# Luna attention and a SmeLU feed-forward on one core: query parts ahead of the values, batch 1's first keys ahead of the weights, orders set anew

## The chip, the core and the metric

One core of one Trainium2 chip runs the whole program. The metric is the device time of one execution in microseconds (us), the median of several. Six engines or queues matter here: TensorE (PE in the profile, with its weight loads as PEld), VectorE (DVE), ScalarE (ACT), GpSimd (POOL), SyncE (SP), and the DMA engines that POOL and SP feed.

## The reference, cut to what matters

```python
def sm_attn(qq, kk, vv):
    s = scale * np.matmul(qq, kk.transpose(0, 1, 3, 2))
    a = np.exp(s - np.max(s, axis=-1, keepdims=True))
    return np.matmul(a / (np.sum(a, axis=-1, keepdims=True) + 1e-09), vv)
p_packed = sm_attn(p, k, v)               # 32 pack queries over 576 keys
out = sm_attn(q, p_packed, p_packed)      # 576 queries over 32 packed keys
x = out.transpose(0, 2, 1, 3).reshape(B * S, H * D)      # 4608 x 512
h = x @ w_in                                             # 512 x 2048
g = np.where(h >= 1, h, np.where(h <= -1, 0.0, (h + 1) ** 2 / 4))
return g @ w_out                                         # 2048 x 512
```

There are 8 batches of 8 heads, 576 tokens, 64 wide. Inputs and output are float32; the kernel multiplies in bfloat16.

## The kernel before, in words

**Tiling.** A batch goes through two stages. The attention stage turns the keys (line 432, tile `tp`, copied to `kT`), takes the scores of the 32 pack queries (line 459, `sp`), their exponentials on ACT (line 462, `ex`), and packs the values (lines 479 and 485, `pk`; from it `ppT` and the reciprocals `rs`). Then come the scores of the real queries against the packed keys (`s`, line 513, and for batch 0 line 591), their exponentials `eT`, the sums `sm` by a matmul with blocks of ones (lines 528 and 597), the inverse of the sums as `ln` and then `rc` on ACT, and the weights `A` on DVE. The packed values are multiplied into `w_in` beforehand: `M` is `ppT` times a block of columns of `w_in` (line 659, tile `mp`, cast to `M` by DVE or ACT), so that a hidden tile of 128 features is `h = M x A` (line 733). The SmeLU of a hidden tile is three instructions: `x` out of PSUM on ACT (line 738), a clamp on DVE (line 743) or ACT (line 745), and a product into `hT` on DVE (line 748). The output tile `o` of 128 tokens sums 16 matmuls of `hT` with `w_out` (line 795); two batches make a pair of 9 output tiles.

**Batch 0** is done in smaller pieces, since everything waits for it: its queries are turned on PE in four pieces (line 582), by x (first or second part of the tokens) and g (four heads each); the hidden tiles whose number is in `HALVED` are made for each half of the tokens apart, the second half with a key that is `hx` later; `MERGED` names the x for which `ln` and `rc` of both g are one instruction; `SPLIT` names the blocks of `M` that are cast in two pieces. The first output tiles of the first pair are summed in two parts (`CUTS`): after that many of the 16 hidden tiles the sum is copied out (`part`, "parked") and added to the rest later (line 806).

**What sets the order.** A planner (`Plan`, `run`, `choose`) writes the instructions out for every engine. It has a cost for each kind of work (`C`), and among the tasks that can start it takes the one with the smallest key; the keys of a hidden tile are its batch plus a sixteenth for each tile, those of the attention work stand in the table `KEYS`, a row for each batch, and output tiles come last (100 and more). Its choice of engine for a copy (DVE or ACT) also follows its costs. On the chip each engine runs its list in order and waits where an input isn't there. Where the planner sees PE with nothing to do before the third output tile, it writes matmuls of zeros (line 870, 512 or 256 columns) into the list: they are work without a result.

**Loads.** POOL issues all input loads in one list: first those of `FIRST` (k, v and queries of batch 0, in parts), then those of `ORDER`, where `r` is the second query part of batch 0, `i` and a number a block of columns of `w_in`, `o` and a number a quarter of `w_out`, `k`, `q` and `v` loads of batch 1, `p` the rest of the pack queries. SP issues the stores of the output and, for later batches, transposes of q and k by DMA.

**PSUM** has three places `W` that everything but the output tiles passes through, and two places `O` for output tiles.

Of the kernel before, what the change touches and what calls it, by code (L numbers as in the profile page):

```python
# [13 lines left out]
         Tca=1.12, Tcd=0.75, ex=0.807, ppo=0.4, ppT=0.41, ppa=0.4, ppd=0.22, rs=0.165,  # L14
         eT=0.741, ln=0.651, rc=0.683, A=0.816, Mca=1.014, Mcd=1.223, x=0.651, ta=0.681, td=0.459, hT=0.757, oba=0.586, obd=0.69, hx=2.181,
         array=0.2, tell=0.04, lead=0.12, until=18.0, feed=0.2374, margin=0.3641, slack=0.1788, wake=1.2, warm=7.0, early=0.2216, wait=0.002722, p4=999.0, bk=115.3)
OVER = {"ACT": 0.104, "DVE": 0.083}
NW, NO, NX, NB = 3, 2, 5, 6
DW, FILL = 256, 512
CUTS = (4, 4, 8, 8)  # L20
PARTS = len(CUTS)

ORDER = 'r i0 i1 i4 o0 i2 q0 i3 k1 k0 o1 v q1 o2 o3 p'

FIRSTS = "kT0 kT1 sc0 sc1 pk0 pk1 q00 q01 q10 q11 s200 s201 s210 s211 sm00 sm01 sm10 sm11 M0 M1 M2 M3 M4".split()
UNITS = "kT0 kT1 qT0 qT1 sc0 sc1 pk0 pk1 s20 s21 sm0 sm1 M0 M1 M2 M3".split()
KEYS = [
# [187 lines left out]
def kernel(  # L215
# [10 lines left out]
    nc = tc.nc  # L226
# [9 lines left out]
    P = 128  # L236
# [10 lines left out]
    X = 2  # L247
# [20 lines left out]
    PE, ACT, DVE, DMA, SP = "PE", "ACT", "DVE", "DMA", "SP"  # L268
# [144 lines left out]
    def attention(b, key):  # L413
# [156 lines left out]
        def first_weights(deps, r):  # L570
# [37 lines left out]
            for x in range(X):  # L608
                boxes, own, cps = [{}, {}, {}], None, []
                for g in range(G):  # L610
                    t = add(PE, C["tp"] * 6, key["q%d%d" % (x, g)], [part_of["q", x, g]] + ([own] if g else []),
                            lambda x=x, g=g, bx=boxes[0]: turn(x, g, bx), takes=None if g else "W", readers=0 if g else 2, mode=1)
                    own = own or t
                    cps.append(both(lambda eng, x=x, g=g, bx=boxes[0]: copy(qT()[:, x, g * w:(g + 1) * w], bx["tp"][:, g, :w])(eng),
                                    C["Tca"] * 0.55, C["Tcd"] * 0.55, key["q%d%d" % (x, g)], [t], frees=own))
                    tq[x, g] = t
                own = None
                for g in range(G):
                    ky = key["s2%d%d" % (x, g)]
# [4 lines left out]
                    eTs[x, g] = add(ACT, C["eT"] * 0.6, ky, [t, r[g]], lambda eng, x=x, g=g, bx=boxes[1]: nc.scalar.activation(  # L624
                        eT(g)[:, x], bx["s2"][:, g, :HALF], AF.Exp, scale=rs()[:, g, 1:]), frees=own)
# [9 lines left out]
                for gs in ([slice(G)] if merged else [slice(g, g + 1) for g in range(G)]):  # L635
# [3 lines left out]
                    for g in range(G)[gs]:  # L639
                        As[x, g] = add(DVE, C["A"] * 0.56, key["sm%d%d" % (x, g)], made, lambda eng, x=x, g=g, bx=bx: nc.vector.scalar_tensor_tensor(  # L640
                            A()[:, g, x], eT(g)[:, x], rs()[:, g, :1], bx["rc"][:, g], ALU.mult, ALU.mult))
# [7 lines left out]
        def mk(f, deps):  # L649
# [15 lines left out]
            war = K.get((b - 2, "h"), [])  # L665
            part = {2: 0.56, 4: 1.0}[n // P] * (0.58 if len(gs) > 1 else 1.0)
            yield t, [both(lambda eng, g=g: copy(M()[:, g, cs], box["mp"][:, g, :n])(eng), C["Mca"] * part,
# [49 lines left out]
    def hidden_tile(b, fi, key, hs=None):  # L717
# [8 lines left out]
        xs = slice(hs[0], hs[-1] + 1)  # L726
        pa, pd = (1.0, 1.0) if n == X else (0.6, 0.56)

# [26 lines left out]
        war = [step_of[b // 2 - 1, i, fi] for i in range(lo, lo + 5)] if b > 1 else []  # L755
        t_ = add(DVE, C["hT"] * pd, key, [t_] + war, third, frees=x_)
        for x in hs:
# [143 lines left out]
```

## Time and profile before

| | before |
|---|---|
| median of 3 runs | 248.5 us (247.53 to 248.61) |
| the profiled execution's own time | 248.8 us |
| its span, first to last instruction | 247.0 us |
| mean granted TensorE clock | 0.979 |
| PE busy | 239.4 us (97%), 2221 matmuls |
| DVE busy, ACT busy | 175.3 us (71%), 185.2 us (75%) |
| POOL busy | 31.3 us (13%) |
| chain that ended last | PE 93%, DMA 3%, POOL, DVE and issue 1% each |

A busy PE is not a useful PE: the matmuls of zeros count as busy, and the ends of matmuls are modelled. So the page's 97% is read together with the groups by line (how many matmuls of zeros there are) and with the timeline of the first 30 us. Windows give the busy time of every engine in a stretch and the granted clock; rows of the timeline give start, duration, engine, line, tiles, count, and in brackets the idle time ahead and what ended it. The chain of waits, in order of time, gives the pieces on which the end hung.

### The profile page before, as it was taken

Reading aid. Unit: us, or ns where it says so; the run is one execution under the profiler, and the core shown is the slowest. Engines: PE = TensorE matmul, PEld = TensorE weight load, DVE = VectorE, ACT = ScalarE, POOL = GpSimd, SP = SyncE. Lnnn points to the kernel's source line nnn. Section 1 sums busy time; section 2 is a strip of 40 time slices with the busy share of each in tenths; the row PEclk is TensorE's granted clock in tenths of the full one; section 3 lists DMA queues with packets and bytes.
Section 4 is the critical chain, followed back from the end, with each engine's and each line's share of the span. In section 5 each row is a group of like instructions: output and inputs, shape, how many; then the busy total and the mean of one; then the engine's idle time right before and its main releaser. Section 6 shows DMA issues by size and latency. Waiting matters only on the chain.

```text
span 247.0 us, 5472 instructions
## 1 busy us (share of the span) xinstructions
PE 239.4 (97%) x2221; PEld 138.0 (56%) x2221; DVE 175.3 (71%) x314; ACT 185.2 (75%) x310; POOL 31.3 (13%) x46
## 2 busy tenths in 40 slices
PE   7689999999999999999999999999999999999994
PEld 2544567467644666357745664576545674476443
DVE  5336999689964699339987995389752997589400
ACT  3328998889967796769998997699466995899410
POOL 8652431210110102002101110000000000000000
PEclk9956999999999999999999999999999999999999
DMA  7999999999999999999999999634433102210232
GB/s 105 170 201 205 204 204 202 198 232 201 192 196 185 204 130 168 180 168 203 181 166 147 197 155 178 137 74 84 90 93 85 42 3 73 57 44 3 60 110 86
DMA packets 57258, 34.67 MB, mean 140 GB/s; under 512 B 30224, under 2 KB 52752, under 8 KB 57232
## 3 DMA queue, kind: packets, MB, share of 16 engines
q0 software_dynamic: 25984, 18.55, 53.2%
q1 hardware_dynamic: 31104, 15.70, 35.1%
q8 instruction: 17, 0.28, 0.5%
q10 hardware_dynamic: 144, 0.07, 0.1%
q14 instruction: 9, 0.07, 0.1%
HBM read 37.22 MB, written 9.44 MB: 189 GB/s over the span
## 4 chain that ended last, share of the span: by engine, by line
PE 93%; DMA 3%; POOL 1%; issue 1%; DVE 1%; ACT 0%; POOLq 0%
PE o L795 51%; PE h L733 26%; PE mp L659 4%; DMA v<-in_v_dram 3%; PE pk L479 2%; PE sp L459 2%; PE tp L432 1%; PE sm L528 1%; PE o L870 1%; PE s L513 1%; PE pk L485 1%; PE tp L582 1%; PE s L591 1%; PE sm L597 0%; POOL k L293 0%
## 5 line engine op out<-in xcount | busy, mean ns | idle before, releaser
L795 PE MATMUL o<-w_out_sb,hT 128*128 128x512 bf16 (+2 forms) x592 | 143.7, 374 | 0.0
L748 DVE SCALAR_TENSOR_TENSOR hT<-x 128x576 bf16<-128x576 f32 (+1 forms) x131 | 90.4, 737 | 0.6
L795 PEld LDWEIGHTS <-hT 128*128 128x128 bf16 x592 | 54.9, 98 | 53.9 <-issue 5.3
L738 ACT ACTIVATE x<-h 128x576 f32<-128x576 f32 (+1 forms) x131 | 76.5, 653 | 7.0 <-PE h L733 6.7
L733 PE MATMUL h<-A,M 128*128 128x288 bf16 x512 | 75.4, 287 | 0.0
L733 PEld LDWEIGHTS <-M 128*128 128x128 bf16 x512 | 49.9, 98 | 22.6 <-issue 1.3
L743 DVE TENSOR_SCALAR x<-x 128x576 f32<-128x576 f32 (+1 forms) x75 | 31.8, 450 | 9.8 <-ACT x L738 9.7
L745 ACT ACTIVATE x<-x 128x576 f32<-128x576 f32 (+1 forms) x56 | 37.5, 697 | 0.1
L375 DVE CAST M<-mp 128x1024 bf16<-128x1024 f32 (+1 forms) x16 | 17.9, 1122 | 13.3 <-PE mp L659 11.0
L375 ACT COPY ob<-o 128x512 f32<-128x512 f32 (+1 forms) x19 | 10.9, 575 | 20.7 <-PE o L795 20.2
L375 DVE COPY ob<-o 128x512 f32<-128x512 f32 (+1 forms) x14 | 9.5, 679 | 20.4 <-PE o L795 20.3
L375 ACT CAST M<-mp 128x1024 bf16<-128x1024 f32 (+2 forms) x20 | 17.6, 912 | 6.8 <-PE mp L659 6.5
L462 ACT ACTIVATE ex<-sp 96x768 bf16<-96x768 f32 x16 | 13.0, 815 | 4.0 <-PE sp L459 4.0
L548 DVE SCALAR_TENSOR_TENSOR A<-eT,rs,rc 128x576 bf16<-128x576 bf16 x12 | 9.8, 816 | 8.0 <-ACT rc L538 8.0
L293 POOL DMA_DIRECT2D k<-in_k_dram x10 | 7.6, 764 | 49.9 <-DMA kT<-k 36.8
L523 ACT ACTIVATE eT<-s,rs 128x576 bf16<-128x576 f32 x14 | 9.8, 746 | 2.7 <-PE s L513 2.4
L293 POOL DMA_DIRECT2D q<-in_q_dram x8 | 6.2, 777 | 42.6 <-DMA qT<-q 21.7
L533 ACT ACTIVATE ln<-sm 128x576 f32<-128x576 f32 x14 | 9.1, 652 | 3.1 <-PE sm L528 2.9
L870 PE MATMUL o<-zeros 128*128 128x512 bf16 (+1 forms) x25 | 10.2, 503 | 1.2 <-DVE zeros L281 1.2
L659 PE MATMUL mp<-w_in_sb,ppT 64*32 64x512 bf16 (+1 forms) x264 | 10.8, 380 | 0.0
L538 ACT ACTIVATE rc<-ln 128x576 f32<-128x576 f32 x14 | 9.6, 682 | 0.4
L459 PEld LDWEIGHTS <-kT 128*128 128x128 bf16 x192 | 7.8, 98 | 2.5 <-DVE kT L375 0.2
(61 smaller groups left out, 129.5 us busy)
## 6 DMA issues: line engine op xcount, KB each, us to landing
out_dram<-ob SPq DMA_DIRECT2D x23, 192.0 KB, 2.9
v<-in_v_dram POOLq DMA_DIRECT2D x7, 576.0 KB, 15.6
k<-in_k_dram POOLq DMA_DIRECT2D x6, 576.0 KB, 16.4
q<-in_q_dram POOLq DMA_DIRECT2D x6, 576.0 KB, 12.1
out_dram<-ob SPq DMA_DIRECT2D x22, 128.0 KB, 3.6
w_out_sb<-in_moe_w_out_dram POOLq DMA_DIRECT2D x4, 512.0 KB, 16.9
w_in_sb<-in_moe_w_in_dram POOLq DMA_DIRECT2D x3, 512.0 KB, 13.2
out_dram<-ob SPq DMA_DIRECT2D x22, 64.0 KB, 2.4
```

The costliest lines, as they stand in the source:

```text
L293: nc.gpsimd.dma_start(tok[nm, b][:, hs].rearrange("p h c d -> p h (c d)"), SRC[nm][b, hs].rearrange("h (p c) d -> p h (c d)", c=NC))
L375: return lambda eng: nc.vector.tensor_copy(out_, in_) if eng == DVE else nc.scalar.copy(out_, in_)
L459: nc.tensor.matmul(o[:, :, a], kT()[:, i, w:w + P], pT[:, b, h], start=True, stop=True)
L462: nc.scalar.activation(ex()[:, :, i].rearrange("p e x a n -> p e (x a n)"), box["sp"], AF.Exp, scale=scale)
L659: nc.tensor.matmul(mp[a * NP:(a + 1) * NP, g, :n], pp_of(y, h), w_in_sb[y * D:(y + 1) * D, h // 2, cs], start=True, stop=True)
L733: nc.tensor.matmul(h[:, hf, :HALF], T[b, "M"][:, g, fi * P:(fi + 1) * P], T[b, "A"][:, g, hf], start=(g == 0), stop=(g == G - 1))
L738: nc.scalar.activation(box["x"], box["h"][:, xs, :HALF], AF.Prelu, bias=-1.0, alpha=0.5)
L743: nc.vector.tensor_scalar(x, x, 1.0, 0.0, ALU.add, ALU.max)
L745: nc.scalar.activation(x, x, AF.Relu, bias=1.0)
L748: nc.vector.scalar_tensor_tensor(hT[:, fi, col + xs.start * HALF:col + xs.stop * HALF].rearrange("p (a t) -> p a t", a=n), box["x"], 1.0, ...
L795: nc.tensor.matmul(box["o", j, part][:, :cs.stop - cs.start], hT[:, fi, i * P:(i + 1) * P], w_out_sb[:, fi, cs], start=(fi == 0 or fi in c ...
L870: plan.run(lambda w: nc.tensor.matmul(o[:, :w], zeros[:, :P], zeros[:, :w], start=True, stop=True))
```

## The change

It changes numbers and tables, and the planner then writes other lists.

- `FIRST`: the two first query parts are loaded between k and v instead of after v.
- `ORDER`: the first half of batch 1's keys (`k0`) is loaded ahead of the first block of `w_in`; batch 1's other key half, its queries and two quarters of `w_out` change places further on.
- `CUTS`: output tiles 2 and 3 are parked after seven hidden tiles instead of eight.
- `HALVED`: a fourth hidden tile of batch 0 is made in halves. `hx`: the second halves have a key of 48 instead of 2 more, behind all other hidden tiles.
- `MERGED`: `ln` and `rc` of the first part of the tokens are made for each g apart. `SPLIT`: only the first block of `M` is cast in two pieces.
- Planner numbers: `feed`, `margin`, `slack`, `early`, `wait`, and the costs of pieces (0.55 to 0.6, 0.6 to 0.675 and so on); all of `KEYS`.

```diff
-         ... hx=2.181,
-         ... feed=0.2374, margin=0.3641, slack=0.1788, ..., early=0.2216, wait=0.002722, p4=999.0, bk=115.3)
+         ... hx=48.25,
+         ... feed=0.2568, margin=0.2281, slack=0.3077, ..., early=0.2764, wait=0.01662, p4=999.0, bk=999.0)
-CUTS = (4, 4, 8, 8)
+CUTS = (4, 4, 7, 7)
-ORDER = 'r i0 i1 i4 o0 i2 q0 i3 k1 k0 o1 v q1 o2 o3 p'
+ORDER = 'r k0 i0 i1 i4 o0 i2 k1 i3 o1 v q0 o2 q1 o3 p'
 KEYS = [
-    [3.797, -2.654, -2.321, 4.058, -3.234, -2.701, ...
+    [-3.469, -3.796, -3.804, -6.263, -4.244, -5.278, ...
...
-SPLIT = ((0, 0), (0, 1), (0, 2))
+SPLIT = ((0, 0),)
-FIRST = "k0 k1 v0 v1 q00 q01"
+FIRST = "k0 k1 q00 q01 v0 v1"
-FLOW = {"k0": 1.48, "k1": 1.52, "v0": 1.5, "v1": 1.46, "q00": 0.8, "q01": 0.8, "r": 1.6, "in0": 2.25, "in1": 1.33}
+FLOW = {"k0": 1.48, "k1": 1.52, "q00": 0.8, "q01": 0.8, "v0": 1.5, "v1": 1.46, "r": 1.56, "in0": 1.5, "in1": 2.0}
-HALVED = (0, 1, 2)
-MERGED = (0, 1)
+HALVED = (0, 1, 2, 3)
+MERGED = (1,)
...
-                                    C["Tca"] * 0.55, C["Tcd"] * 0.55, key["q%d%d" % (x, g)], [t], frees=own))
+                                    C["Tca"] * 0.6, C["Tcd"] * 0.6, key["q%d%d" % (x, g)], [t], frees=own))
...
-        pa, pd = (1.0, 1.0) if n == X else (0.6, 0.56)
+        pa, pd = (1.0, 1.0) if n == X else (0.63, 0.62)
```

The lists themselves move most at the start. First POOL, which issues the loads, from the first loads to the first block of `w_in` (a minus is the list before, a plus the new one; line 293 loads k or v, line 340 a query part, `masks.py` builds the identity for the transposes):

```order
 L293 DMA k<-in_k_dram 96x4x384 x2
-L293 DMA v<-in_v_dram 96x4x384
+L340 DMA q<-in_q_dram 96x4x192
 masks.py:197 MEMSET ident 128x128
 masks.py:199 ISA
 masks.py:199 AFFINE_SELECT ident<-ident 128x128
-L293 DMA v<-in_v_dram 96x4x384
-L340 DMA q<-in_q_dram 96x4x192 x2
+L340 DMA q<-in_q_dram 96x4x192
+L293 DMA v<-in_v_dram 96x4x384 x2
 L340 DMA q<-in_q_dram 96x8x192
+L293 DMA k<-in_k_dram 96x4x384
```

The two query parts pass the two value halves, and a key half of batch 1 now stands ahead of the first weights.

Then ACT, from batch 0's exponentials of the real scores to its first hidden tiles. Before (numbers tell the tiles apart):

```order
L624 ACTIVATE eT_301<-s2_285,rs_227 128x288
L602 ACTIVATE ln_332<-sm_299 128x576
L624 ACTIVATE eT_292<-s2_334,rs_227 128x288
L624 ACTIVATE eT_301<-s2_334,rs_227 128x288
L607 ACTIVATE rc_349<-ln_332 128x576
L375 CAST M_362<-mp_352 128x256
L602 ACTIVATE ln_365<-sm_347 128x576
L607 ACTIVATE rc_381<-ln_365 128x576
L375 CAST M_362<-mp_372 128x256
L738 ACTIVATE x_392<-h_384 128x288
```

And now:

```order
L602 ACTIVATE ln_337<-sm_333 128x288
L607 ACTIVATE rc_344<-ln_337 128x288
L624 ACTIVATE eT_293<-s2_339,rs_256 128x288
L602 ACTIVATE ln_337<-sm_333 128x288
L624 ACTIVATE eT_318<-s2_339,rs_256 128x288
L607 ACTIVATE rc_344<-ln_337 128x288
L602 ACTIVATE ln_385<-sm_371 128x576
L375 CAST M_401<-mp_375 128x256
L607 ACTIVATE rc_404<-ln_385 128x576
L462 ACTIVATE ex_413<-sp_387 96x3x256
L738 ACTIVATE x_417<-h_407 128x288
```

`ln` and `rc` of the first part stand there twice, half as wide, and the exponential of batch 1's first scores (`ex_413`) stands ahead of the first hidden tile's `x`.

Last DVE, from batch 0's turned queries to its weights `A`:

```order
-L375 COPY qT_95<-tp 128x576 x4
-L375 CAST M<-mp 128x256
-L640 SCALAR_TENSOR_TENSOR A<-eT,rs,rc 128x288 x2
+L375 COPY qT_95<-tp 128x576 x2
+L640 SCALAR_TENSOR_TENSOR A<-eT,rs,rc 128x288
+L375 COPY kT_94<-tp 128x1152
+L640 SCALAR_TENSOR_TENSOR A<-eT,rs,rc 128x288
 L375 CAST M<-mp 128x256
 L640 SCALAR_TENSOR_TENSOR A<-eT,rs,rc 128x288 x2
```

The copy of batch 1's first turned keys (`kT_94`) now stands between the two weights `A` of the first part; the other two query copies went ahead, behind batch 0's own keys.

On PE the matmuls are the same but for zeros: before there are 20 of 512 and 5 of 256 columns, now 23 and 4. Up to the place where PE makes three whole hidden tiles of batch 0 in a row (12 matmuls of line 733) for the first time, it now also has 12 transposes of batch 1's keys (line 432) and 12 of its scores (line 459), and one output matmul (line 795) less. Batch 0's first query transposes (24 of line 582) stand ahead of its second scores; before they stood behind both `pk`.

More of the change, by code (lines that the diff above doesn't have):

```diff
@@ L14 @@
          Tca=1.12, Tcd=0.75, ex=0.807, ppo=0.4, ppT=0.41, ppa=0.4, ppd=0.22, rs=0.165,
-         eT=0.741, ln=0.651, rc=0.683, A=0.816, Mca=1.014, Mcd=1.223, x=0.651, ta=0.681, td=0.459, hT=0.757, oba=0.586, obd=0.69, hx=2.181,
-         array=0.2, tell=0.04, lead=0.12, until=18.0, feed=0.2374, margin=0.3641, slack=0.1788, wake=1.2, warm=7.0, early=0.2216, wait=0.002722, p4=999.0, bk=115.3)
+         eT=0.741, ln=0.651, rc=0.683, A=0.816, Mca=1.014, Mcd=1.223, x=0.651, ta=0.681, td=0.459, hT=0.757, oba=0.586, obd=0.69, hx=48.25,
+         array=0.2, tell=0.04, lead=0.12, until=18.0, feed=0.2568, margin=0.2281, slack=0.3077, wake=1.2, warm=7.0, early=0.2764, wait=0.01662, p4=999.0, bk=999.0)
 OVER = {"ACT": 0.104, "DVE": 0.083}
@@ L623, in first_weights @@
                     K.setdefault((b, "s2"), []).append(t)
-                    eTs[x, g] = add(ACT, C["eT"] * 0.6, ky, [t, r[g]], lambda eng, x=x, g=g, bx=boxes[1]: nc.scalar.activation(
+                    eTs[x, g] = add(ACT, C["eT"] * 0.675, ky, [t, r[g]], lambda eng, x=x, g=g, bx=boxes[1]: nc.scalar.activation(
                         eT(g)[:, x], bx["s2"][:, g, :HALF], AF.Exp, scale=rs()[:, g, 1:]), frees=own)
@@ L639, in first_weights @@
                     for g in range(G)[gs]:
-                        As[x, g] = add(DVE, C["A"] * 0.56, key["sm%d%d" % (x, g)], made, lambda eng, x=x, g=g, bx=bx: nc.vector.scalar_tensor_tensor(
+                        As[x, g] = add(DVE, C["A"] * 0.63, key["sm%d%d" % (x, g)], made, lambda eng, x=x, g=g, bx=bx: nc.vector.scalar_tensor_tensor(
                             A()[:, g, x], eT(g)[:, x], rs()[:, g, :1], bx["rc"][:, g], ALU.mult, ALU.mult))
@@ L665, in mk @@
             war = K.get((b - 2, "h"), [])
-            part = {2: 0.56, 4: 1.0}[n // P] * (0.58 if len(gs) > 1 else 1.0)
+            part = {2: 0.57, 4: 1.0}[n // P] * (0.63 if len(gs) > 1 else 1.0)
             yield t, [both(lambda eng, g=g: copy(M()[:, g, cs], box["mp"][:, g, :n])(eng), C["Mca"] * part,
@@ L755, in hidden_tile @@
         war = [step_of[b // 2 - 1, i, fi] for i in range(lo, lo + 5)] if b > 1 else []
-        t_ = add(DVE, C["hT"] * pd, key, [t_] + war, third, frees=x_)
+        t_ = add(DVE, C["hT"] * (1.0 if n == X else 0.59), key, [t_] + war, third, frees=x_)
         for x in hs:
```

16 rows, old and new, of the table KEYS are left out of this document.

## The prediction

> **What bounds the kernel now.** I read the page's first part, then the busy times by stretch, cut at the places where the granted clock changes, then the chain of waits of the first 40 us.
>
> ```profile
> PE 239.4 (97%) x2221; PEld 138.0 (56%) x2221; DVE 175.3 (71%) x314; ACT 185.2 (75%) x310; POOL 31.3 (13%) x46
> ```
>
> ```profile
> 6.10:9.50 3.40, 2.43 (x50) 1.92 (x47) 1.65 (x4) 1.05 (x2) 2.87 (x4) 1.00 1.22 157
> 9.50:12.90 3.40, 2.20 (x50) 1.57 (x50) 0.94 (x6) 1.06 (x3) 1.90 (x3) 1.00 1.50 186
> 12.90:16.30 3.40, 2.65 (x29) 1.38 (x30) 1.17 (x3) 0.97 (x2) 1.86 (x4) 0.50 1.46 199
> 16.30:19.70 3.40, 3.20 (x44) 1.56 (x40) 0.82 (x2) 1.75 (x5) 1.26 (x2) 0.50 1.25 205
> 19.70:23.10 3.40, 3.40 (x26) 1.27 (x19) 2.69 (x7) 3.02 (x7) 1.26 (x2) 0.50 1.25 207
> 23.10:26.50 3.40, 3.40 (x29) 1.90 (x28) 3.37 (x7) 2.76 (x8) 0.99 (x2) 0.99 1.27 203
> 26.50:30.00 3.50, 3.50 (x30) 2.07 (x29) 3.47 (x9) 3.39 (x8) 1.59 (x2) 1.00 1.29 205
> 30.00:40.00 10.00, 10.00 (x116) 6.79 (x114) 9.80 (x17) 9.45 (x16) 3.45 (x5) 1.00 1.28 205
> 50.00:244.00 194.00, 193.86 (x1722) 112.72 (x1716) 140.52 (x238) 151.71 (x252) 9.61 (x12) 1.00 0.80 129
> ```
>
> The columns are the stretch, its length, PE, PEld, DVE, ACT, POOL, the granted clock, the DMA share and GB/s. From 50 us on PE is busy 193.86 of 194.00 us: no order of the same matmuls can win more than the missing 0.14 us there. What can be won lies ahead, where PE waits or multiplies zeros. Those are counted by group:
>
> ```profile
> L870 PE MATMUL o<-zeros 128*128 128x512 bf16 x20 | 9.0, 539 | 1.2 <-DVE zeros L281 1.2
> L870 PE MATMUL o<-zeros 128*128 128x256 bf16 x5 | 1.8, 360 | 0.0
> ```
>
> The chain tells where the last zeros end and what pieces cost (start, duration, what):
>
> ```profile
> 11.47 0.52 PE pk L479 x12
> 12.84 0.32 DVE ppT L375
> 15.36 0.43 PE s L591 x4
> 16.14 1.12 PE tp L582 x24
> 20.28 0.85 PE o L870 x2
> 25.56 0.65 PE o L870 x3
> 26.43 1.57 PE h L733 x12
> 34.75 0.51 PE tp L432 x12
> 37.34 0.41 PE sp L459 x12
> 39.03 0.43 PE o L795 x2
> ```
>
> I take one place in both lists: the first three whole hidden tiles in a row, at 26.43 us here. Behind it PE has no zeros left and is full, so the end of the program moves as this place moves, less the useful work that was added ahead of it. That work is 12 transposes (0.51) and 12 scores (0.41) of batch 1, less one output matmul (0.43 / 2 = 0.22): **0.70 us**, which PE need not do later. So the change in time is (new place - 26.43) - 0.70.
>
> **The loads.** The waits of the timeline show when a load is there:
>
> ```profile
> 9.99 0.41 PEld L479 LDWEIGHTS <-v 96*128 96x128 bf16 x12 [0.92 <-DMA v<-in_v_dram]
> 13.02 0.13 PEld L582 LDWEIGHTS <-q 96*64 96x64 bf16 x1 [0.31 <-DMA q<-in_q_dram]
> 14.80 0.68 POOL L293 DMA_DIRECT2D k<-in_k_dram  x1 [0.79 <-DMA q<-in_q_dram]
> 16.13 0.68 POOL L293 DMA_DIRECT2D k<-in_k_dram  x1 [0.65 <-DMA w_in_sb<-in_moe_w_in_dram]
> 17.85 0.75 POOL L326 DMA_DIRECT2D w_out_sb<-in_moe_w_out_dram  x1 [1.04 <-DMA w_in_sb<-in_moe_w_in_dram]
> 20.04 0.79 POOL L293 DMA_DIRECT2D v<-in_v_dram  x1 [1.44 <-DMA w_in_sb<-in_moe_w_in_dram]
> ```
>
> Two query parts are as many bytes as one value half. So the first value half now comes when the second did, at about 11.5 (the `pk` row at 11.47), and the second when the last of these six did, at 13.0. The last query part stays at about 14.5. Batch 1's first key half takes the place of the first `w_in` block, 16, and every block behind it comes one such half, 1.5 us, later: 17.3, 19.1 and 21.3 instead of 15.8, 17.6 and 19.8. PE asks for them at about 19.5, 21.9 and 25 (worked out below), so this delay lies under the softmax of batch 0 and costs nothing; were that cover gone, it would cost 1.5 us. The second scores now wait for the second query part, at the latest 9.9, when a value half came before. Their exponential (0.80) then ends near 11.7, ahead of the values it is for (13.0): also nothing.
>
> **The chain of batch 0.** From the second value half: before, `pk` began at 11.47 and `ppT` was complete at 12.84 + 0.32 = 13.16, 1.69 later, at full clock. Now 13.0 + 1.7, and 0.4 more since the 18 matmuls of `pk` (0.5 to 0.6 together) run at the half clock that stands from 12.9 on: 15.1. The zeros placed ahead of the second `s` (two of 512, one of 256; 0.43 for 512 by the row at 20.28, so 1.07) end near 15.2 and hide under it. Then `s` at 15.2 (15.36 before), and the 24 query transposes (1.12) from 15.6 to 16.7; the first `sm` gives the first `ln` at about 17.0. From here ACT is never idle by its list. Its durations:
>
> ```profile
> 17.63 0.65 ACT L602 ACTIVATE ln<-sm 128x576 f32<-128x576 f32 x1 [1.30 <-PE sm L597]
> 22.33 0.74 ACT L738 ACTIVATE x<-h 128x288 f32<-128x288 f32 x2
> ```
>
> ```profile
> L738 ACT ACTIVATE x<-h 128x288 f32<-128x288 f32 x6 | 2.3, 413 | 0.5 <-PE h L733 0.5
> L624 ACT ACTIVATE eT<-s,rs 128x288 bf16<-128x288 f32 x4 | 1.9, 499 | 3.3 <-PE s L591 3.3
> L602 ACT ACTIVATE ln<-sm 128x576 f32<-128x576 f32 x2 | 1.3, 652 | 1.3 <-PE sm L597 1.3
> L607 ACT ACTIVATE rc<-ln 128x576 f32<-128x576 f32 x2 | 1.4, 682 | 0.0
> L462 ACT ACTIVATE ex<-sp 96x768 bf16<-96x768 f32 x5 | 4.0, 804 | 2.4 <-PE sp L459 2.4
> L375 ACT CAST M<-mp 128x256 bf16<-128x256 f32 x2 | 0.7, 373 | 0.3 <-DVE M L375 0.3
> L375 ACT CAST M<-mp 128x512 bf16<-128x512 f32 x2 | 1.1, 618 | 0.0
> L375 ACT CAST M<-mp 128x1024 bf16<-128x1024 f32 x3 | 3.0, 1017 | 1.8 <-PE mp L659 1.8
> L745 ACT ACTIVATE x<-x 128x288 f32<-128x288 f32 x2 | 0.9, 453 | 0.0
> ```
>
> A half-wide `ln` or `rc` isn't in the trace. Its bounds are half of the whole (0.33) and the whole (0.68); nearest are the other half-wide instructions on ACT (0.41 and 0.50), so 0.43. Ahead of the first `x` stand four of these and two `eT` (4 x 0.43 + 2 x 0.50 = 2.72), then `ln`, a cast, `rc` and batch 1's `ex` (0.65 + 0.37 + 0.68 + 0.80 = 2.50): the first `x` at 17.0 + 5.2, less 0.2 of overlap, is **22.0, against 22.33**. The 0.6 us won at `ln` (17.63 before) is half spent on the two extra instructions and on `ex`, which before ran much later. Behind it stand two `x` (0.74), the cast of the second block (0.62), four `x` (1.48), a clamp (0.45) and the cast of a 512 block (1.02): 4.3, less 0.3 of overlap where the next doesn't depend on the last (the pair at 22.33 took 0.74, not 0.83), and 0.3 for places in PSUM, since each of these hidden halves needs one that an `x` has just left. So the block that the whole tiles need is cast at 26.3 and the place is at **26.4**, as before. By the bounds of the half-wide ones it could be 26.0 to 27.4.
>
> That place holds only if PE isn't behind ACT. Three matmuls of zeros stand ahead of the second block's `mp`: at full clock 0.65 (row at 25.56), at half clock 1.28. The first two hidden halves end near 21.3 at full clock, `mp` is then done at 22.4, and ACT asks for it at 22.7. I take it that the clock is back by then: in this trace it came back after the first stretch in which PE was full (3.40 of 3.40), not after 2.65 or 3.20. The new list puts `pk`, two `s`, two and a half zeros and most of 24 transposes into 12.9 to 16.3, where there were half a `tp`, two `s`, one `sm` and under two zeros, and scores, keys and a zero into the next stretch; so it comes back one or two stretches of 3.4 us earlier.
>
> The Trainium skill (TensorE: Matmul & The Clock Gate, What's actually happening) says that the clock gate judges free-running windows of 3413 ns and grants the full clock after one busy window. The stretches of this trace, 3.4 us long, agree with the length; by that rule the new list would regain the clock at 16.3 or 19.7. The same section's table lets the clock fall only after an idle window; here it fell behind a stretch in which PE was busy 2.20 of 3.40 us, so the measurement decides.
>
> **Sum.** 26.4 - 26.43 - 0.70 = -0.7 us. The profiled execution took 248.8, its span 247.0; the 1.8 around the span stays. So a span of 246.3, and against the median of 248.5: **247.8 us**.
>
> **What costs nothing.** Parks at seven and the new key for parked sums move the same copies and additions; the cover is the output work of the other tiles, and at worst two output matmuls (0.43) must wait. The fourth halved tile adds 2 x 0.41 - 0.65 = 0.17 on ACT and, by the same ratio, some 0.3 on DVE, the casts in one piece give back 2 x 0.62 - 1.02 = 0.22. ACT and DVE are at 9.45 and 9.80 of 10 us between 30 and 40, so what is left over (about 0.3 on each, with the second `ln` and `rc`) can reach PE; I leave it to the range. The new keys of batches 2 to 7 and SP's swapped places can cost but not win, by the 0.14 above.
>
> **The rivals.**
> 1. *The clock comes back at 23.1 as before.* For it: 3.20 of 3.40 wasn't enough at 16.3 to 19.7. Then the three zeros take 1.28, and with the slower hidden halves before them `mp` comes 0.7 later; ACT waits, and the place is at 27.1: 27.1 - 26.43 - 0.70 = 0.0, **248.5**.
> 2. *The clock doesn't fall at 12.9.* For it: five zeros now stand around the first `pk`, where there were two. Against it: the gaps until the loads come remain. Then `pk` loses its 0.4, the transposes take 0.5 instead of 1.12, and the first `ln` waits only for the second `eT`, 15.7; the place is 1.3 earlier than in the sum, 25.1: **246.5**.
> 3. *ACT and DVE fall behind and PE waits for them* (slower). Batch 1's `ex` stands ahead of every `x` on ACT, and needs PE's scores, which need DVE's copy of the keys:
> ```profile
> L375 DVE COPY kT<-tp 128x1152 bf16<-128x1152 bf16 x2 | 1.5, 758 | 0.0
> ```
>    By the sum the keys are turned at 18.7, copied at 19.5, scored at 20.5, and ACT asks at 21.2, so it decides from 0.7 us of lateness on; behind it stand all `x`, and no zeros or output matmuls can fill PE. With the half clock of rival 1, a delay of the copy behind `A` (0.5 each), and the 0.3 left over, the place comes 0.5 + 0.5 + 0.3 = 1.3 behind that of rival 1: 248.5 + 1.3 = **249.8**. Against it: loads and the copy have slack by the rows.
>
> That the tables do nothing is excluded for the start by the lists.
>
> **How the numbers follow.** Forecast 0.42 (its own range 247.1 to 248.6), rival 1 0.25, rival 2 0.15, rival 3 0.18. A measurement tells about 0.5% (1.24 us) from no change. Faster than 247.26 are rival 2 and the lower part of the forecast: 0.15 + 0.13 = 0.28. Slower than 249.74 are some four fifths of rival 3: 0.15. The rest, 0.57, is within 0.5%. The range reaches from rival 2 to rival 3: 246.4 to 249.8.
>
> **What would show it.** The second `pk` near 13.0, the second `s` near 15.2, the first `ln` near 17.0, the first `x` near 22.0, whole hidden tiles at 26.4, the clock at 1.00 before 20, and no idle PE behind. A clock at 0.50 up to 23 is rival 1, one at 1.00 throughout rival 2, an idle PE between 22 and 45 rival 3. Wrong altogether would be a gain or loss behind 50 us.

## The result and the profile after

The changed kernel takes 246.86 us (median of 9 executions, 245.84 to 247.97), the kernel before 248.61 in the same comparison (9 executions, 247.53 to 249.04). The ratio is 0.9929, with a 95% interval of 0.991 to 0.9948: some 1.75 us faster, where 0.7 was forecast. The time lies inside the stated range (246.4 to 249.8), but below the forecast's own (247.1 to 248.6) and nearest to rival 2 (246.5). The profiled execution has the median time, 246.86, and a span of 245.1 (247.0 before).

The chain of waits of the changed kernel, from the second `pk` to the place that the prediction watched (start, duration, what):

```profile
13.71 0.35 PE pk L479 x12
...
14.90 0.20 DVE ppT L375
15.15 0.30 PE s L591 x4
15.45 0.63 PE tp L582 x24
...
16.47 0.42 ACT ln L602
...
20.75 0.69 ACT ex L462
21.44 0.59 ACT x L738 x2
22.03 0.48 ACT M L375
...
24.26 0.81 PE o L870 x3
25.07 1.59 PE h L733 x12
```

The second score starts 0.05 us behind the end of `ppT` (15.15 against 14.90 + 0.20); before it was 2.20 behind (15.36 against 12.84 + 0.32), with a query copy, 12 transposes, the first score and its exponential in between. The place is at 25.07 instead of 26.43.

The busy times by stretch (stretch, length, PE, PEld, DVE, ACT, POOL, granted clock, DMA share, GB/s), cut as those of before:

```profile
9.50:12.90 3.40, 3.18 (x56) 2.62 (x54) 1.16 (x3) 1.05 (x3) 2.27 (x4) 1.00 1.43 197
12.90:16.30 3.40, 3.32 (x58) 1.88 (x56) 1.25 (x7) 1.48 (x4) 0.78 (x2) 1.00 1.40 199
...
19.70:23.10 3.40, 3.10 (x24) 1.46 (x23) 2.34 (x7) 3.31 (x9) 0.79 (x2) 1.00 1.24 207
```

The clock column says 1.00 everywhere. That isn't so for the first stretch, as PE's timeline shows (start, duration, engine, line, what, count, and in brackets the idle time ahead):

```profile
11.41 0.63 PE L870 MATMUL o<-zeros 128*128 128x512 bf16 x1 [0.22 <-issue]
...
12.68 1.03 PE L870 MATMUL o<-zeros 128*128 128x512 bf16 x3
...
19.40 0.38 PE L870 MATMUL o<-zeros 128*128 128x512 bf16 x1
```

One matmul of zeros takes 0.63 at 11.41 but 0.38 at 19.40, and three take 1.03 across 13 us but 0.81 at 24.26 (the chain above). The trace has no record of the clock before 13.15 us, where it becomes full, and the stretches without a record count as full. So PE ran at half rate up to 13.15, and from there at full rate to the end; the half clock that the kernel before had from 12.9 to 23.2 is not there behind 13.15.

### The profile page after: what moved, and what is told of

Its sections match the earlier page's. It is cut to its first block, busy times and chain, and to the rows that moved or that the text cites. A ratio compares the mean times of both kernels' runs of the same rounds, so it can differ in the third digit from the quotient of the medians.

```text
span 245.1 us, 5440 instructions
## 1 busy us (share of the span) xinstructions
PE 236.3 (96%) x2185; PEld 138.8 (57%) x2223; DVE 172.8 (71%) x312; ACT 187.0 (76%) x315; POOL 31.0 (13%) x46
## 3 DMA queue, kind: packets, MB, share of 16 engines
q1 hardware_dynamic: 31104, 15.70, 34.5%
## 4 chain that ended last, share of the span: by engine, by line
PE 92%; ACT 2%; DMA 2%; issue 2%; DVE 1%; POOL 0%; POOLq 0%
PE o L795 50%; PE h L733 26%; PE mp L659 3%; PE sp L459 2%; PE pk L479 2%; DMA k<-in_k_dram 2%; PE tp L432 2%; PE sm L528 1%; PE s L513 1%; PE o L870 1%; PE pk L485 1%; PE tp L582 1%; ACT rc L607 1%; ACT eT L624 0%; ACT M L375 0%
## 5 line engine op out<-in xcount | busy, mean ns | idle before, releaser
L795 PE MATMUL o<-w_out_sb,hT 128*128 128x512 bf16 (+2 forms) x557 | 137.2, 373 | 2.1 <-issue 0.9
L738 ACT ACTIVATE x<-h 128x576 f32<-128x576 f32 (+1 forms) x132 | 77.8, 664 | 3.1 <-PE h L733 2.6
L743 DVE TENSOR_SCALAR x<-x 128x576 f32<-128x576 f32 (+1 forms) x78 | 33.0, 450 | 11.6 <-ACT x L738 11.5
L375 ACT COPY ob<-o 128x512 f32<-128x512 f32 (+1 forms) x22 | 12.8, 581 | 18.8 <-PE o L795 17.4
L375 DVE CAST M<-mp 128x1024 bf16<-128x1024 f32 (+1 forms) x14 | 16.3, 1166 | 12.7 <-PE mp L659 12.6
L375 ACT CAST M<-mp 128x1024 bf16<-128x1024 f32 (+2 forms) x20 | 18.5, 962 | 6.5 <-PE mp L659 6.3
L375 DVE COPY ob<-o 128x512 f32<-128x512 f32 (+1 forms) x11 | 7.4, 677 | 15.0 <-PE o L795 14.8
L293 POOL DMA_DIRECT2D v<-in_v_dram x9 | 7.0, 782 | 26.1 <-PE pk L485 23.6
L870 PE MATMUL o<-zeros 128*128 128x512 bf16 (+1 forms) x24 | 8.6, 474 | 1.5 <-DVE zeros L281 1.2
## 6 DMA issues: line engine op xcount, KB each, us to landing
v<-in_v_dram POOLq DMA_DIRECT2D x7, 576.0 KB, 14.1
k<-in_k_dram POOLq DMA_DIRECT2D x6, 576.0 KB, 13.5
w_in_sb<-in_moe_w_in_dram POOLq DMA_DIRECT2D x3, 512.0 KB, 15.6
```

The lines of the kernel that those rows point to most:

```text
L293: nc.gpsimd.dma_start(tok[nm, b][:, hs].rearrange("p h c d -> p h (c d)"), SRC[nm][b, hs].rearrange("h (p c) d -> p h (c d)", c=NC))
L375: return lambda eng: nc.vector.tensor_copy(out_, in_) if eng == DVE else nc.scalar.copy(out_, in_)
L738: nc.scalar.activation(box["x"], box["h"][:, xs, :HALF], AF.Prelu, bias=-1.0, alpha=0.5)
L743: nc.vector.tensor_scalar(x, x, 1.0, 0.0, ALU.add, ALU.max)
L795: nc.tensor.matmul(box["o", j, part][:, :cs.stop - cs.start], hT[:, fi, i * P:(i + 1) * P], w_out_sb[:, fi, cs], start=(fi == 0 or fi in c ...
L870: plan.run(lambda w: nc.tensor.matmul(o[:, :w], zeros[:, :P], zeros[:, :w], start=True, stop=True))
```

## The experiments

All are compared with the kernel before, run beside them. "Before" below means that kernel, "changed" the one predicted.

| | what runs | median us (executions) | ratio to before, 95% interval |
|---|---|---|---|
| | changed | 246.86 (9) | 0.9929 [0.9910, 0.9948] |
| e1 | before, 7 zeros ahead of `pk` | 248.16 (10) | 1.0003 [0.9981, 1.0024] |
| e2 | changed, 17 zeros fewer | 247.10 (10) | 0.9953 [0.9936, 0.9970] |
| e3 | before, new `FIRST` | 247.08 (10) | 0.9942 [0.9918, 0.9966] |
| e4 | changed, old `ORDER` | 251.03 (4) | 1.0120 [1.0081, 1.0160] |
| e5 | changed, old `FIRST` | 253.23 (4) | 1.0211 [1.0168, 1.0254] |
| e6 | changed, old keys for batches 2 to 7 | 246.04 (5) | 0.9908 [0.9875, 0.9942] |
| e7 | before, clock held by 10 zeros | 247.49 (10) | 0.9978 [0.9950, 1.0005] |
| e8 | before, new `FIRST` and `ORDER` | 250.79 (4) | 1.0097 [1.0065, 1.0128] |
| e9 | before, new order of the loads, old lists | 249.60 (6) | 1.0051 [1.0032, 1.0070] |
| e10 | e3 with 3 zeros more | 245.94 (6) | 0.9907 [0.9879, 0.9935] |
| e11 | e6 with 3 zeros fewer | 246.13 (6) | 0.9905 [0.9879, 0.9931] |
| e12 | e6 with one zero wider | 246.30 (12) | 0.9924 [0.9897, 0.9952] |

Two theories stood at the start. By the first, the gain over the forecast is the clock, which fell in the kernel before and didn't in the changed one. By the second, the new order of the first loads takes the query transposes off the way between `ppT` and the second score.

**e1: zeros in the kernel before.**

```diff
             def mm():
+                if b == 0:
+                    for _ in range((4, 3)[gs[0]]):
+                        zero(FILL)
                 pk = wide([P, 1024], f32, "pk")
```

> The kernel before with its lists unchanged, but four matmuls of zeros (512 columns) put on PE ahead of batch 0's first packed values and three ahead of the second. The computation stays whole. Theory clock (most of the gain is that the TensorE clock, once full, isn't lowered again at 12.9 us): PE is now full in the two waits for the value halves, the clock stays at 1.00 from its first rise on, the first three whole hidden tiles in a row begin about 1 us earlier (25.3 to 25.6 instead of 26.43) and the time is 0.8 to 1.2 us shorter than before, 247.4 to 247.8. Theory order (the gain is the 0.70 us of batch 1's work that was moved ahead, and the earlier loads): zeros add nothing useful; the time is that of before or up to 0.5 us longer, 248.5 to 249.1.

It was 248.16, no difference. But in the profiled execution the zeros didn't hold the clock; they only put its fall off, from 12.92 to 15.36. The stretches, cut where that profile's clock changes (it rises at 5.12 and falls at 15.36) and every 3.41 us between:

```profile
5.12:8.54 3.42, 2.04 (x40) 1.47 (x38) 1.55 (x5) 0.58 (x1) 3.42 (x6) 1.00 1.29 195
...
11.95:15.36 3.41, 2.31 (x45) 1.43 (x41) 1.53 (x5) 0.79 (x3) 1.81 (x3) 1.00 1.49 196
15.36:18.78 3.42, 3.22 (x37) 1.68 (x36) 0.82 (x2) 1.88 (x4) 1.42 (x2) 0.50 1.27 207
```

Behind 3.41 us with PE busy 2.31 the clock is halved at 15.36 and stays so to 22.19. So the profile doesn't test what a held clock is worth. The ten executions speak rather against a large price: the four with a mean clock of 0.999 or more have a median of 248.16, the three at 0.986 one of 247.96.

**e2: the changed kernel without 17 of its zeros**, all behind the first ten.

```diff
+    def zero(w):
+        made.append(w)
+        if len(made) - 1 not in range(10, 27):
+            nc.tensor.matmul(o[:, :w], zeros[:, :P], zeros[:, :w], start=True, stop=True)
-    plan.run(lambda w: nc.tensor.matmul(...))
+    plan.run(zero)
```

> The changed kernel with its lists unchanged, but without the 17 matmuls of zeros from the wait for the first packed values on. The computation stays whole. Theory clock: without them PE is idle for a good part of 11 to 25 us, the clock rises late or falls again, and the time goes up by 0.7 to 1.5 us from the changed kernel's 246.9, to 247.6 to 248.4. Theory order: the zeros only stand in PE's way (in the profile of the changed kernel three of them end 1.5 us after the second value half has landed), so without them it is 0.3 to 0.8 us faster, 246.1 to 246.6.

It was 247.10, within the scatter of the changed kernel, though its profile has the half clock from 7.65 to 21.31 us. From its stretches and its chain:

```profile
16.30:19.70 3.40, 3.40 (x40) 1.83 (x39) 2.32 (x6) 2.82 (x7) 2.13 (x3) 0.50 1.31 204
```

```profile
12.49 0.82 PE pk L479 x12
...
14.90 1.10 PE tp L582 x24
...
25.23 1.65 PE h L733 x12
```

The 24 transposes take 1.10 instead of 0.63, but the second `pk`, with no zeros ahead of it, begins 1.2 earlier than the row at 13.71 above, and the place is at 25.23, 0.16 later. In this profile zeros and clock about cancel; neither theory had foreseen that. The ten executions agree: the five with a mean clock of 0.972 have a median of 247.01, the five that read 1.00 one of 247.20.

**e3: the kernel before with the new order of the first loads**, and no other edit; the planner writes all lists anew.

```diff
-FIRST = "k0 k1 v0 v1 q00 q01"
+FIRST = "k0 k1 q00 q01 v0 v1"
```

> The kernel before with the new order of the first loads alone (both first query parts between k and v); the planner writes the rest anew with the old keys and costs. Theory loads (the query parts between k and v make the second value half and all behind it land 1 us earlier, as the two profiles show): the second value half lands near 12.0 and the time is 0.5 to 1.0 us shorter than before. Theory clock: it depends on whether the clock falls, which its zeros (28 instead of 25, five around the first packed values) make less likely; if it holds, 0.8 to 1.2 shorter, if not, within 0.3 of before.

It was 247.08: of the 1.75 us this one line brings about 1.45 (0.9942 of 248.6). From the chain and the timeline:

```profile
13.65 0.20 DVE ppT L375
13.89 0.30 PE s L591 x4
...
14.43 0.65 PE tp L582 x24
...
23.03 1.65 PE h L733 x12
```

```profile
34.97 0.65 PE L733 MATMUL h<-A,M 128*128 128x288 bf16 x4 [0.43 <-DVE kT L375]
```

The second score is 0.04 behind `ppT`, as in the changed kernel, and the three whole tiles start at 23.03, 2.0 earlier than there. It doesn't keep all of this lead: ahead of this row PE stands still for 0.43 us, for DVE's copy of batch 1's keys. The changed kernel, with one half of that copying done before 20 us, has no wait there.

The 1.45 us are not the load order alone. The new list has three zeros more, and this profile's clock is full from 6.48 us on, while it fell in the kernel before. Among executions with a mean clock of 0.99 or more, the eight of e3 have a median of 246.78, the eleven of the kernel before (beside e1 to e12) one of 247.60: 0.8 apart. So the clock may be part of the 1.45.

**e9: the order of the loads alone.** The planner is told the old order, so every engine's list but POOL's stays as it was.

```diff
-        for n, nm in enumerate(FIRST.split()):
+        for n, nm in enumerate("k0 k1 q00 q01 v0 v1".split()):
             if n == IDENT:
```

> The kernel before with the six first loads issued in the new order (k k q q v v) and every engine's list as it was. The theory that the gain of FIRST is the list that it permits (query transposes and their copies off the way between ppT and the second score) and that the order of the loads by itself only makes the values later: pk starts at 10.8 and 12.3 instead of 10.0 and 11.5, ppT is complete 0.7 later, the second score still about 1.8 behind it; 248.9 to 249.6. The rival that the early landing of the queries is the gain: 247.5 or less.

It was 249.60, 1.2 slower, as the first theory of that run said. Its chain:

```profile
14.12 0.19 DVE ppT L375
14.34 0.47 DVE qT L375
14.85 0.69 PE tp L582 x12
15.54 0.39 PE s L591 x4
...
16.50 0.43 PE s L591 x4
```

The queries are there, but DVE and PE still turn them behind `ppT`: the second score is 2.2 behind it. `ppT` itself is complete 1.15 later than before, since the second value half lands 0.97 later (12.40 against 11.43) and the second `pk` takes 0.82 instead of 0.52. The last is the clock, which in this profile is half from 8.72 to 22.37 us, so part of the 1.2 may be the clock's. What the run does show is that the loads alone win nothing: the gain of e3 needs the list that the new order permits, and that list has to make up for the later values first.

**e7: the clock held in the kernel before**, with e1's zeros and three more.

```diff
             def turn(x, g, box):
+                if (x, g) == (0, 1):
+                    zero(FILL)
+                    zero(FILL)
 ...
             def inner(x, g, box):
+                if (x, g) == (0, 1):
+                    zero(FILL)
```

> The kernel before with matmuls of zeros in PE's idle time up to 15 us (four ahead of the first pk, three ahead of the second, two ahead of the second half of the first query transposes, one ahead of the second score); what is computed is whole. The theory that the half clock costs the kernel before about 0.9 us and that an idle stretch brings it: the clock isn't halved before 18 us, and the time is 247.3 to 248.0 against 248.6. The rival that the chain up to the first ln is made of DVE copies and waits that don't follow PE's clock: 248.4 to 248.9, the first ln still behind 17.0. If the clock falls at 13 to 16 us with PE busy, idle time isn't what brings it.

It was 247.49. By the medians that is 1.1 below before (248.58), by the ratio 0.5, and with one execution at 250.26 the interval reaches 1.0005, so by itself it doesn't settle the matter. The mean clock is at 0.998 or above in all ten executions, so it didn't fall for long; that it rose early is seen only in the profiled one, whose matmuls are at full rate from 5.86 us on. Its chain, and its place in PE's timeline:

```profile
12.60 0.20 DVE ppT L375
12.83 0.47 DVE qT L375
13.34 0.45 PE tp L588 x12
...
14.62 0.30 PE s L599 x4
```

```profile
24.42 1.64 PE L741 MATMUL h<-A,M 128*128 128x288 bf16 x12 [0.23 <-ACT x L746]
```

The way from `ppT` to the second score is still 1.8 us long: the queries weren't moved. The place is 2.0 earlier than before; the span is 1.3 shorter. That the clock is worth about 1.1 us there has a second witness, though one that was only observed: of the 69 executions of the kernel before that ran beside e1 to e12, the 44 with a mean clock below 0.98 have a median of 248.69, the 11 at 0.99 or more one of 247.60. An execution whose loads land early could be faster and hold its clock for the same reason, and e1's executions show no such difference, so 1.1 us is an estimate and not a measured price.

**e10: both**, e3 with one zero ahead of each `pk` and one ahead of the third score.

```diff
-FIRST = "k0 k1 v0 v1 q00 q01"
+FIRST = "k0 k1 q00 q01 v0 v1"
 ...
             def mm():
+                if b == 0:
+                    zero(FILL)
                 pk = wide([P, 1024], f32, "pk")
 ...
             def inner(x, g, box):
+                if (x, g) == (1, 0):
+                    zero(FILL)
```

> The kernel before with FIRST alone (247.1) and three more matmuls of zeros (one ahead of each pk, one ahead of the third score); what is computed is whole. The theory that the clock (1.1 us by holding it in the kernel before) and the load order are two gains: 246.0 to 246.6. The rival that they are the same time won twice, since the list with FIRST no longer waits on PE at half rate: 246.9 to 247.4.

It was 245.94, 0.9907 of before, or 2.3 us less (2.5 by the medians): near the sum of e3 and e7, which is 1.45 + 0.55 = 2.0 by the ratios and 1.3 + 1.1 = 2.4 by the medians. The mean clock is at 0.998 or above in all six executions; in e3 it was below that in four of ten. From the chain:

```profile
13.51 0.20 DVE ppT L375
...
13.75 0.30 PE s L595 x4
...
22.88 1.64 PE h L737 x12
```

That fits two gains that add up, better than one gain won twice (246.9 or more was expected for that). It isn't shown that the second gain is the clock: e3's own profile was at full clock too, and its eight executions with a mean clock of 0.99 or more (246.78) are 0.8 above this one; and the intervals of e3 and e10 overlap. This kernel has the lowest median of all. It beats the kernel before clearly, but its interval (0.9879 to 0.9935) overlaps that of the changed kernel.

**e5: the changed kernel with the old `FIRST`.** The diff is e3's, turned round.

```diff
-FIRST = "k0 k1 q00 q01 v0 v1"
+FIRST = "k0 k1 v0 v1 q00 q01"
```

> The changed kernel with the old load order alone (k k v v q q); ORDER, MERGED, keys and all else as changed. The theory that the gain is made by the two query parts passing the values: their transposes and copies stand again between the completion of ppT and the second score, so that score comes 1.5 to 2 us behind ppT (0.06 us in the changed kernel, 2.2 us in the kernel before), the first ln about 1.2 us later than 16.5, and three whole hidden tiles in a row start at 26 or later; the time is 248.0 or more. The rival that the rest of the change (batch 1's keys ahead, the orders on ACT and DVE, the keys) carries a good part of the gain: 247.5 or less, with the first ln late all the same.

It was 253.23. The time fits the first theory of that run, but the reason given for it does only in part: the first `ln` is at 15.6, earlier than in the changed kernel. The second score does come 1.8 behind `ppT`, as that theory said, but the place is at 25.57, only 0.5 later, while the time is 6.4 longer. PE loses its time far behind the start. The stretch from 60 us of e5, and what PE waits for from 40 to 120 us (us, times, longest):

```profile
60.00:70.00 10.00, 8.43 (x95) 5.17 (x95) 7.64 (x13) 9.64 (x15) 0.77 (x1) 1.00 1.31 192
```

```profile
PE o L795 <- DVE hT L748: 1.5, 4, 0.9
```

and the same stretch of the changed kernel:

```profile
60.00:70.00 10.00, 9.89 (x109) 5.97 (x117) 8.32 (x16) 8.16 (x14) 1.54 (x2) 1.00 1.30 178
```

The output matmuls there wait for hidden tiles of batch 1, and ACT is at 9.64 of 10 us. Another load order let the planner write another list, in which the elementwise work of batches 0 and 1 piles up. So e5 can't say what `FIRST` is worth in the changed kernel.

**e4 and e8: the order of the later loads.** e4 is the changed kernel with the old `ORDER`; e8 is e3 with the new one.

```diff
-ORDER = 'r k0 i0 i1 i4 o0 i2 k1 i3 o1 v q0 o2 q1 o3 p'
+ORDER = 'r i0 i1 i4 o0 i2 q0 i3 k1 k0 o1 v q1 o2 o3 p'
```

> The changed kernel with the old order of the later loads alone (batch 1's first key half behind the weights again). So the 12 transposes and 12 scores of batch 1 are no longer ahead of the first whole hidden tiles. Theory of the sum (useful work moved into the waits, worth 0.70 us): 0.5 to 0.9 us slower than the changed kernel, 247.4 to 247.8. Rival (w_in then comes 1.5 us earlier, ACT has no exponential of batch 1 ahead of the first hidden tile, and the place comes as much earlier): within 0.3 us of the changed kernel. Theory clock, if nothing but the clock mattered: also no change as long as the mean clock stays near 1.0.

> The kernel before with both load orders changed (FIRST and ORDER) and the old keys, CUTS, HALVED, MERGED. The theory that the query parts' load order makes the gain and ORDER nothing by itself: 246.6 to 247.6, as with FIRST alone (247.1). The rival that ORDER and the new keys only do together what each spoils alone: 249 or more with the old keys, with PE idle between 55 and 120 us. A third: batch 1's keys ahead add to the gain: 246.3 or less.

They were 251.03 and 250.79: 4.2 above the changed kernel, and 3.7 above e3. The chain of waits from 55 to 80 us says where, in its shares by line; first e4, then the changed kernel:

```profile
by line: PE o L795 43.4%; DVE hT L748 32.4%; DVE x L743 7.4%; PE sp L459 5.7%; PE pk L479 2.8%; DVE ob L806 2.4%; ACT x L745 2.3%; PE sm L528 2.0%; PE s L513 1.5%; PE pk L485 1.1%; PE mp L659 0.9%; issue 0.3%
```

```profile
by line: PE o L795 59.7%; PE h L733 23.0%; PE mp L659 3.9%; PE pk L479 2.8%; PE sp L459 2.8%; PE tp L432 2.0%; PE sm L528 2.0%; issue 1.7%; PE s L513 1.5%; PE pk L485 1.1%
```

In the changed kernel the chain stays on PE there, in e4 DVE sets the pace of the hidden tiles, as in e5. In e8 DVE's `hT` is 40.4% of the same stretch, in e3 it is no part of the chain. So `ORDER` and the rest of the change go together, and either alone costs about 4 us. In e4 all of it is lost behind the place, which is at 22.5 there; in e8 more than half is. Which part of the rest it is (the keys of batches 0 and 1, `CUTS`, `HALVED`, `MERGED` or the planner's numbers) no run tells apart; by e6 below it isn't the late keys. Together they cost nothing that shows, and I have no run in which they win.

**e6: the old keys for batches 2 to 7** (six rows of numbers in the changed kernel, the start's list unchanged).

```diff
-    [2.111, 0.613, 3.000, 0.548, ...
+    [-0.971, -1.257, 7.656, 0.403, ...
 ... and so the five rows below it
```

> The changed kernel with the old keys for batches 2 to 7; the start is the same list. The theory that nothing is won behind 50 us: within 0.4 us of the changed kernel, 246.5 to 247.3. The rival that the late keys belong to the load order and are needed to keep the gain (as the old ORDER lost 3.4 us of PE time behind 55 us): 249 or more, with stalls between 55 and 120 us.

It was 246.04, with an interval that overlaps the changed kernel's. The late keys win nothing; whether they cost some tenths can't be told from this.

**e11 and e12: is the start of the changed kernel still bound by PE's rate?** Both build on e6. e11 was meant to leave out the three zeros ahead of the second `pk`. By its trace it leaves out one of the two ahead of the first `pk` and two of those three, and one still stands at 12.43. (The changed kernel's trace has records of 24 of its 27 matmuls of zeros, so they can't be counted by these alone; their 27 weight loads are all there.) e12 makes the seventh zero 512 columns wide instead of 256, so that PE opens as in the kernel before.

```diff
+        if len(made) - 1 not in (11, 12, 13):      # e11
+            nc.tensor.matmul(o[:, :w], zeros[:, :P], zeros[:, :w], start=True, stop=True)
 ...
+        w = FILL if len(made) == 7 else w          # e12
+        nc.tensor.matmul(o[:, :w], zeros[:, :P], zeros[:, :w], start=True, stop=True)
```

> The changed kernel with the old keys for batches 2 to 7 (246.0) and without the three matmuls of zeros ahead of the second pk, which in the changed kernel's profile ran at half rate and held that pk up until 13.5, 1.5 us behind the landing of its values; what is computed is whole. The theory that these zeros cost what they hold up: the second pk starts at 12.4 to 12.8, ppT is complete at 14.4 and the first ln at 15.8 to 16.0; 245.3 to 245.7. The rival that without them the clock comes back one stretch of 3.4 us later and gives it back: the first ln at 16.4 or later and 245.9 to 246.4.

> The changed kernel with the old keys for batches 2 to 7 (246.0) whose seventh matmul of zeros has 512 columns instead of 256, so that the first seven are those of the kernel before and PE has no idle 0.2 us behind them. In the three profiles of the changed kernel's list where the clock came up only behind 12.9 us, that gap is there; in the seven profiles that open with seven of 512 it came up by 6.5 us. The theory that this gap decides and that the changed kernel's start still pays for half clock: clock up by 6.5 us, the second pk at 12.0 to 12.5, the first ln at 15.3 to 15.8, and 245.0 to 245.6. The rival that the start isn't set by PE's rate there: 245.8 to 246.4, with the clock up early. A third, that the gap has nothing to do with it: the clock up behind 12 us again.

They were 246.13 and 246.30, against e6's 246.04: no gain. In e11 the clock came up at 13.48 and the start did move, yet only by 0.4 at the place. Its chain:

```profile
13.02 0.62 PE pk L479 x12
...
15.03 0.63 PE tp L582 x24
...
24.65 1.59 PE h L733 x12
```

In e12 it was up from 4.81, and another thing came last; its chain:

```profile
5.93 8.89 DMA q<-in_q_dram
...
14.87 0.70 PE tp L582 x24
...
24.56 1.59 PE h L733 x12
```

The query transposes waited for the last query part, which landed at 14.83. In this list an earlier `pk` or a full clock wins at most 0.5 at the place, and none of it shows in the medians.

## Why the prediction came out as it did

The forecast was a gain of 0.7 us by moved work, with the place where it was. Both kernels' profiles confirm the way of counting: 25.07 - 26.43 - 0.70 = -2.06, and the span fell by 1.9. What was wrong is the place, 26.4 against 25.07, by two terms of the sum. So the time fell where rival 2 had put it; a time below 247.26 had been given a chance of 0.28. The two profiles also differ by scatter: in the one before, the last of the first six loads landed at 12.98, in three others with the same load order (e1, e5, e7) at 11.91 to 12.57. Part of the 1.36 us between the places may be that.

- **The chain up to `ppT` and the second `s`: right.** Forecast 15.1 and 15.2, measured 15.10 and 15.15. That is in part luck, since errors cancelled: the values landed 1.0 earlier than the 13.0 assumed (the last of the six loads at 11.97), but PE, at half rate, had its zeros ahead of the second `pk` and came to it at 13.5; and from there the clock was full, so the 0.4 added for half clock wasn't paid.
- **The 24 transposes at half clock: mis-sized.** 1.12 was taken and 0.63 measured, since the clock didn't fall after all. So the first `ln` came at 16.47 instead of 17.0.
- **ACT from the first `ln` to the first `x`: right.** Forecast 5.0; 16.47 to 21.34 is 4.87. The half-wide `ln` and `rc` took 0.41 and 0.44, the estimate was 0.43.
- **ACT from the first `x` to the cast of the block: mis-sized by 0.7.** 4.3 was taken (22.0 to 26.3); ACT's timeline says 3.62:

```profile
21.34 0.70 ACT L738 ACTIVATE x<-h 128x288 f32<-128x288 f32 x2
21.91 0.59 ACT L375 CAST M<-mp 128x512 bf16<-128x512 f32 x1
22.38 1.35 ACT L738 ACTIVATE x<-h 128x288 f32<-128x288 f32 x4
23.62 0.44 ACT L745 ACTIVATE x<-x 128x288 f32<-128x288 f32 x1
23.95 1.01 ACT L375 CAST M<-mp 128x1024 bf16<-128x1024 f32 x1
```

  Each instruction starts about 0.1 before the one ahead of it ends: 21.91 + 0.59 = 22.50, and the next begins at 22.38. The sum took 0.3 off for that overlap and put 0.3 on for places in PSUM; nothing of such a wait is seen. It doesn't hang on the clock either: e2, at half clock until 21.31, has about the same distance from the first `x` to the place (3.68 against 3.73).
- **Loads, later `w_in` blocks, parks, `SPLIT`: nothing that shows, as forecast.** No row of PE's waits between 22 and 45 us names a load or an `M`; there is one wait of 0.2. No run tests these parts alone.
- **Rival 2, the clock that doesn't fall: it came nearest,** with 246.5 and a place of 25.1. Only half of its reason is true. In the profile the clock was half up to 13.15 and full behind it, but its price for that was too high and what it left alone (ACT's overlap) made up for it. It put the first `ln` at 15.7, measured 16.47.
- **Rival 1 and rival 3: not seen.** The mechanism of rival 3 is there in e5 and e8, but PE waits for hidden tiles there behind 60 us, not between 22 and 45.
- **"Can cost but not win" behind 50 us: held** for the late keys (e6). What another list at the start can cost behind 50 us had no term in the prediction: e4, e5 and e8 lose about 4 to 6 us.

The sources of the gain were also not those of the forecast. It credited the moved work of batch 1. e3 wins 1.45 us without moving it; e7, with more zeros alone, 0.5 to 1.1. Beside e3, the changed kernel is spared the 0.43 us at 34.5, and its place is later (25.07 against 23.03), which its moved work (0.70) pays back in part. The prediction had the second score's distance from `ppT` among its rows, but priced it only as "15.2 against 15.36", because the later values hid what had left the chain.

How the 1.75 us divide between the load order and the clock is not settled. In the kernel before the two seem to add up (e10), with the clock's part not shown; in the changed kernel's list, neither zeros nor clock moved the median (e2, e11, e12).

## What to carry to other kernels

When a load order is changed, ask what list it permits, not when the bytes land: the same loads cost 1.2 us with the old lists and won 1.45 with new ones, the clock's part in both included. Sum an engine's back-to-back work by the distance from start to start, not by durations. Read the clock from the duration of one known instruction beside the clock column, and when a planner writes the list, look at the stretches far behind the edit before a part of a change is judged alone.

## What the runs showed of the hardware

- **A mean clock of 1.00 can hide half clock at the start.** The record begins with a rise of the clock; the changed kernel ran at half rate for 13.15 us and shows 1.00. The traces of e4 and e7 have no record at all.
- **The busy share of a stretch didn't decide whether the clock fell.** In the traces with a record, the clock's changes lie 3.41 us or a multiple of it apart (3.41 in e5, 13.65 in e2). In e1, cut at that step from its rise, the clock stayed full behind 2.04 us of PE busy and fell behind 2.31. Nor did it decide the rise: e2's clock rose at 4.24 behind 2.96 of 3.41 us, and that of the kernel before stayed half at 19.75 behind 3.21. What decides is open. The Trainium skill (TensorE: Matmul & The Clock Gate, What's actually happening) puts the fall behind at least one idle window. The trace doesn't agree: PE was not idle in the window ahead of e1's fall.
- **When the clock comes up differs with small things at the start.** In the three profiles with a row like the first below (the changed kernel, e6, e11) it came up at 12.9 to 13.5 us; in all those that open as in the second (before, e1, e3, e7 to e10, e12), by 6.5, in e7 by the durations. The first row is of the changed kernel's timeline, the second of e12's:

```profile
4.34 0.64 PE L389 MATMUL tpp<-ident,p_nat 128*64 128x128 bf16 x8 [0.19 <-DVE p_nat L384]
```

```profile
4.34 0.62 PE L389 MATMUL tpp<-ident,p_nat 128*64 128x128 bf16 x8
```

  It isn't the gap of 0.19 alone: e2, e4 and e5 have it too (0.18 or 0.19), and their matmuls are at full rate by 4.8.
- **The same loads land at different times.** The last of the first six was there between 11.9 and 13.0 us over the fourteen profiles, and the last query part at 13.5 to 14.1 in most, at 14.5 in the kernel before and 14.8 in e12.
